# Attention with two mixtures of experts: pinned splits and swaps, value products four head pairs behind the scores

## The chip, the cores and the metric

One core of a Trainium2 chip runs the kernel. Its time is the device time of one execution in microseconds (us); the number for the kernel before is the median of 3 executions. The core has five engines that run at the same time and meet through semaphores: TensorE (PE, matmuls and transposes; its weight loads are shown as PEld), VectorE (DVE), ScalarE (ACT), GpSimd (POOL) and SyncE (SP), which computes nothing and issues DMAs in the order of its queue. TensorE's granted clock is shown as a share of 2.4 GHz; it is either 1.00 or 0.50.

## The reference

```python
# q, k, v: (4, 8, 576, 64); window 128; H = 8 heads, D = 64
scores = scale * q @ k^T                      # per batch and head
scores = where(0 <= i - j < 128, scores - slope[h] * |i - j|, -1e9)
attn = softmax(scores); x = attn @ v          # x becomes (2304, 512)
p = domain_probs / (sum(domain_probs) + 1e-9) # 4 experts, dense
out = sum_e p[:, e] * (relu(x @ w1[e]) @ w2[e])
logits = out @ phi                            # soft mixture: 8 experts, 4 slots each
d = softmax(logits, over tokens); slots = d^T @ out
slot_out[e] = relu(slots[e] @ m1[e]) @ m2[e]
result = softmax(logits, over slots) @ slot_out
```

## The kernel before, in words

The 2304 tokens are 18 tiles of 128. In float16 terms every operand is kept as a high half and a low half (the rounded value and the rest), so that the matmuls run in float16 and keep most of float32's precision.

**Attention, tiles 0 to 17.** For tile i, raw q, k and v (128 x 512, float32) are loaded by SyncE (`ld`, L292). ScalarE writes the high half of q and of k (`sp_qk_hi`, L300), GpSimd the low half (`sp_qk_lo`, L305). The halves lie in one buffer per name (`qs`, `ks`, one buffer each), so the split of the next tile can't begin before the DMA that transposes this tile's has landed. From tile 2 on, that transpose is a DMA issued by SyncE (`tr_q`, `tr_k` and `trans`, L318 to L338; L320 is the issue). qT needs a second copy with its halves exchanged: two VectorE copies (`swap_q`, L339 to L342). Tiles 0 and 1 are transposed by TensorE instead.

The heads go in four pairs per tile; `n = 4 i + hp` is the step of the main loop (L499), and "pair 12.1" below is tile 12, head pair 1. A step computes the scores (`qk`, L349, matmuls of L357 with qT and of L362 with the swapped qT, into one of two PSUM banks, S0 and S1 in turn). Then `soft` (L366): VectorE adds the bias and takes the row's extreme (L374, twice), ScalarE takes the exponential (L379, twice) and writes the high half of the probabilities (L384), GpSimd the low half (L385), and SyncE issues the DMA transpose to eT. `pv` (L392) multiplies eT with v (L402), LAG = 3 steps after the scores. After a tile's fourth pair, `xn` (L405) scales by the row sums, and `xn_c` (L432) splits the result (ACT, POOL) and has it transposed by a DMA into xT, which the first mixture's layer 1 reads.

**The first expert in the gaps.** Between the steps, pieces of the first mixture's expert 0 are put in from a list (`pend`) with a budget of modelled time per step: layer 1 (`l1_piece`, L199) reads xT, VectorE and ScalarE split its result (L213, L214), layer 2 is L227. Tiles 0 and 1 use float32 matmuls (L266, L276).

**After the attention** come the other experts (L634 and L709), then the soft mixture with its own weights and the output.

**What sets the order.** The kernel's text only says what is to be done. A scheduler orders each engine's instructions by the order of the text and by when its own model of time holds them ready, so one engine's order may differ from the text. Each engine then takes its list strictly in that order: an instruction that waits holds up everything behind it on its engine. `tc.issue_after(ins)`, which the change uses, makes instructions of a block stand behind `ins` on `ins`'s engine.

## Time and profile before

| | |
|---|---|
| median of 3 executions | 940.98 us (938.55 to 941.99) |
| the profiled execution | 940.18 us, span 938.3 us |
| mean granted clock of TensorE | 0.983 |
| TensorE busy | 886.7 us of the span (95%) |
| VectorE, ScalarE, GpSimd busy | 566.5, 372.4, 179.9 us |

The page cuts the span into 40 slices of 23.5 us. TensorE is at four and six tenths in the first two slices, at eight in five of the next nine, and at seven in two of the last three. The DMA engines are busy at six tenths or more through the first ten slices and nearly idle from the twelfth to the thirty-first. So there are three parts to read apart: the start and the attention (to about 260 us), the dense experts, and the soft mixture at the end. A busy share alone tells little here; the views that say what TensorE waited for, and when its clock was low, tell more.

### The profile page before, as it was taken

The numbers are of one execution on the slowest core, as the hardware profiler recorded it, in microseconds if no ns is written. First come the engines' busy times: TensorE is split into PE (matmuls) and PEld (weight loads), VectorE is DVE, ScalarE is ACT, GpSimd is POOL, SyncE is SP. The second block draws the span as 40 slices with busy tenths as digits, with TensorE's granted clock in tenths as the row PEclk, the third lists the DMA queues.
The fourth block names the chain that finished last, engine by engine and source line by source line (L and its number), as shares of the span: only waits on it lengthen the run. The fifth ranks groups of instructions, "written<-read, shape, count | busy, mean of one in ns | idle before, by whom it ended". The sixth has DMA issues, their size and how long they took to land.

```text
span 938.3 us, 16272 instructions
## 1 busy us (share of the span) xinstructions
PE 886.7 (95%) x6426; PEld 516.8 (55%) x6426; DVE 566.5 (60%) x1217; ACT 372.4 (40%) x912; POOL 179.9 (19%) x169
## 2 busy tenths in 40 slices
PE   4689898989899999999999999999999999999797
PEld 3566676656765655555555555555555445554432
DVE  7855565547549387657575756666666454556512
ACT  5956766757734243223131323232233201223412
POOL 5555655656520000000000000000000005310000
PEclk9989999999999999999999999999999999999799
DMA  9698998999960110100101010101001008983696
GB/s 261 124 192 157 178 191 174 185 199 152 147 142 24 46 46 3 44 23 23 45 1 45 1 46 1 45 3 44 23 23 46 0 1 303 221 216 133 237 377 241
DMA packets 222028, 102.35 MB, mean 109 GB/s; under 512 B 187216, under 2 KB 201584, under 8 KB 221952
## 3 DMA queue, kind: packets, MB, share of 16 engines
q1 hardware_dynamic: 212320, 78.14, 39.2%
q10 hardware_dynamic: 6800, 13.11, 4.0%
q0 software_dynamic: 2832, 10.07, 2.9%
q8 instruction: 50, 0.82, 0.4%
q14 instruction: 26, 0.21, 0.1%
HBM read 64.59 MB, written 4.72 MB: 74 GB/s over the span
## 4 chain that ended last, share of the span: by engine, by line
PE 75%; DMA 9%; ACT 4%; issue 4%; DVE 4%; POOL 2%; SPq 1%; POOLq 0%; DVEq 0%; ACTq 0%
PE l L709 22%; PE A L634 12%; PE l L199 9%; PE l L227 9%; PE C L634 6%; DMA eT<-e 4%; PE B L634 3%; PE hp L1040 2%; DMA qT<-qs 2%; PE l2f L276 2%; PE so_ps L1058 2%; PE x L402 1%; DMA m<-in_moe_w_dram 1%; ACT e L379 1%; PE fp L1071 1%
## 5 line engine op out<-in xcount | busy, mean ns | idle before, releaser
L709 PE MATMUL l<-w,h 128*128 128x512 f16 x1080 | 252.9, 379 | 0.0
L237 DVE SCALAR_TENSOR_TENSOR acc<-l,pr,acc 128x512 f32<-128x512 f32 x216 | 161.3, 748 | 126.6 <-PE l L709 103.3
L634 PEld LDWEIGHTS <-w 128*128 128x128 f16 x1260 | 123.1, 98 | 94.2
L709 PEld LDWEIGHTS <-h 128*128 128x128 f16 x1080 | 105.5, 98 | 115.3
L199 PE MATMUL l<-xT,w 128*128 128x256 f16 (+2 forms) x1152 | 149.4, 281 | 5.8 <-DMA xT<-xs 3.6
L227 PE MATMUL l<-w,h 128*128 128x512 f16 x600 | 141.9, 383 | 0.7 <-DVE acc L237 0.7
L658 ACT ACTIVATE ct<-A 128x384 f32<-128x384 f32 x90 | 43.5, 487 | 219.0 <-PE A L634 218.9
L199 PEld LDWEIGHTS <-w 128*128 128x128 f16 x1152 | 105.0, 99 | 39.4 <-issue 6.7
L803 POOL DMA_DIRECT2D m<-in_moe_w_dram x19 | 13.7, 723 | 510.2 <-DVE h L654 446.9
L385 POOL TENSOR_TENSOR e<-e,e 128x512 f16<-128x512 f32 (+1 forms) x72 | 80.9, 1130 | 61.8 <-ACT e L384 45.8
L227 PEld LDWEIGHTS <-h 128*128 128x128 f16 x600 | 57.8, 99 | 61.4 <-issue 3.5
L213 ACT ACTIVATE h<-l 128x256 f16<-128x256 f32 (+2 forms) x96 | 36.4, 382 | 110.2 <-PE l L199 75.9
L379 ACT ACTIVATE e<-e,nmx 128x256 f32<-128x256 f32 (+1 forms) x144 | 69.7, 485 | 20.2 <-DVE nmx L374 19.8
L214 DVE SCALAR_TENSOR_TENSOR h<-l,h 128x256 f16<-128x256 f32 (+2 forms) x96 | 40.9, 429 | 59.2 <-ACT h L213 59.0
L634 PE MATMUL C<-xs,w 128*128 128x384 f16 x360 | 71.3, 326 | 0.0
L374 DVE CUSTOM_DVE_ANT_0 e<-s,bias 128x256 f32<-128x256 f32 (+1 forms) x144 | 52.5, 404 | 28.4 <-PE s L362 23.5
L634 PE MATMUL A<-xs,w 128*128 128x384 f16 x360 | 69.3, 326 | 0.0
L634 PE MATMUL A<-xT,w 128*128 128x384 f16 x360 | 67.7, 327 | 0.0
L653 ACT ACTIVATE h<-ct 128x384 f16<-128x384 f32 x90 | 43.8, 515 | 46.5 <-PE l L709 25.1
L357 PE MATMUL s<-kT,qT 128*128 128x128 f16 x272 | 45.4, 228 | 7.7 <-DVE nmx L374 4.6
L654 DVE SCALAR_TENSOR_TENSOR h<-ct,h 128x384 f16<-128x384 f32 x90 | 47.6, 549 | 2.3 <-ACT h L653 2.1
L362 PE MATMUL s<-kT,qT 128*128 128x128 f16 x272 | 44.9, 230 | 4.0 <-DVE qT L342 4.0
(185 smaller groups left out, 993.2 us busy)
## 6 DMA issues: line engine op xcount, KB each, us to landing
m<-in_moe_w_dram ACTq DMA_DIRECT2D x25, 512.0 KB, 5.6
stg<-in_moe_w_dram SPq DMA_DIRECT2D x20, 512.0 KB, 4.9
m<-in_moe_w_dram SPq DMA_DIRECT2D x20, 512.0 KB, 10.2
m<-in_moe_w_dram POOLq DMA_DIRECT2D x19, 512.0 KB, 12.4
stg<-in_moe_w_dram SPq DMA_DIRECT2D x24, 256.0 KB, 3.2
out_dram<-ots SPq DMA_DIRECT2D x18, 256.0 KB, 3.0
qr<-in_q_dram SPq DMA_DIRECT2D x16, 256.0 KB, 3.9
kr<-in_k_dram SPq DMA_DIRECT2D x16, 256.0 KB, 4.3
```

The lines of the kernel that those rows point to most:

```text
L199: nc.tensor.matmul(pt, lhsT=w1_ap(e, fc, wa, kc), rhs=x_ap(t0, n, xa, kc), start=first_mm, stop=(kc == KC - 1 and wa == 1))
L227: nc.tensor.matmul(pt, lhsT=ht[:, ha, o:o + P], rhs=w2_ap(e, fc, wa), start=(fc == fcs[0] and ha == 0 and wa == 0), stop=(fc == fcs[-1] an ...
L237: nc.vector.scalar_tensor_tensor(out=a, in0=pt, scalar=p, in1=a, op0=ALU.mult, op1=ALU.add)
L357: nc.tensor.matmul(o, lhsT=qT[i][:, 0, h], rhs=mv, start=True, stop=False)
L362: nc.tensor.matmul(o, lhsT=qT[i][:, 1, h], rhs=mv, start=False, stop=True)
L374: nc.vector.tensor_tensor_reduce(out=et[:, hl, c0:], in0=st[:, hl, c0:], in1=bias[:, h, c0:], op0=ALU.add, op1=ALU.min, scale=-0.125, scal ...
L379: nc.scalar.activation(out=et[:, hl, c0:], in_=et[:, hl, c0:], func=AF.Exp, scale=-1.0, bias=nmx[i][:, h:h + 1], accum_out=sums[i][:, h:h ...
L385: nc.gpsimd.tensor_tensor(out=e2[:, :, 1], in0=et[:, :, c0:], in1=e2[:, :, 0], op=ALU.subtract)
L634: nc.tensor.matmul(o, lhsT=wq_[:, blk, wa, kc], rhs=xf(xa, kc), start=(first and kc == 0 and wa == 0 and xa == 0), stop=(kc == 1 and wa == 1),
L653: nc.scalar.activation(out=o[:, 0], in_=src, func=AF.Relu)
L654: nc.vector.scalar_tensor_tensor(out=o[:, 1], in0=src, scalar=0.0, in1=o[:, 0], op0=ALU.max, op1=ALU.subtract)
L709: nc.tensor.matmul(pt, lhsT=u["h"][:, z, ha, par, i * P:(i + 1) * P], rhs=w2_ap(e, 2 * qd + z, wa), start=(z == 0 and ha == 0 and wa == 0) ...
```

## The change

The edits, all in the attention stage:

- raw q, k and v share one ring of five buffers (`raw`) in place of two each; the scratch for the bias shares the ring of `e`;
- `soft` becomes three functions, called apart: the scores' extreme, the exponential with the halves, and the transpose;
- q's swap stands behind the extreme of head pair 2 (pinned on VectorE);
- the high half of the next tile's k stands behind the high half of pair 0's probabilities (pinned on ScalarE), one step earlier in the text than before; that of the q of the tile after the next stands behind pair 3's, which is also one step earlier; their low halves on GpSimd follow in the text;
- q's transpose moves from the tile's second step to its first, k's from the third to the second;
- `xn_f` and `xn_c` come at the end of a step; the pieces of the experts alternate with the value products in the text;
- LAG is 4 in place of 3, `e2` has four buffers in place of three, `eT` seven in place of six;
- a finished tile's expert pieces become available one step later.

```diff
-            t = at([P, H, D], F32, nme + "r")
+            t = at([P, H, D], F32, "raw", 5)
...
-    def soft(i, hp, st):
+    def soft_max(i, hp, st):
         kb0 = kbs(i)[0]
         if hp == 0:
             sums[i] = at([P, H], F32, "sums")
             nmx[i] = at([P, H], F32, "nmx")
-        c0, w = kb0 * P, (2 - kb0) * P
-        et = at([P, 2, 2 * P], F32, "e", 3)
+        c0 = kb0 * P
+        et = es[i, hp] = at([P, 2, 2 * P], F32, "e", 3)
         for hl in range(2):
             h = 2 * hp + hl
-            nc.vector.tensor_tensor_reduce(out=et[:, hl, c0:], in0=st[:, hl, c0:], in1=bias[:, h, c0:],
-                                           op0=ALU.add, op1=ALU.min, scale=-0.125, scalar=3.0e38,
-                                           accum_out=nmx[i][:, h:h + 1])
+            mx = nc.vector.tensor_tensor_reduce(out=et[:, hl, c0:], in0=st[:, hl, c0:], in1=bias[:, h, c0:],
+                                                op0=ALU.add, op1=ALU.min, scale=-0.125, scalar=3.0e38,
+                                                accum_out=nmx[i][:, h:h + 1])
+        return mx.ins
+
+    def soft_exp(i, hp):
+        kb0 = kbs(i)[0]
+        c0 = kb0 * P
+        et = es.pop((i, hp))
         for hl in range(2):
             h = 2 * hp + hl
             nc.scalar.activation(out=et[:, hl, c0:], in_=et[:, hl, c0:], func=AF.Exp, scale=-1.0,
                                  bias=nmx[i][:, h:h + 1], accum_out=sums[i][:, h:h + 1])
-        e2 = at([P, 2, 2, 2 * P], F16, "e2", 3)
+        e2 = at([P, 2, 2, 2 * P], F16, "e2", 4)
         if kb0:
             e2 = e2.rearrange("p a b c -> p (a b c)")[:, 0:4 * P].rearrange("p (a b c) -> p a b c", a=2, b=2)
-        nc.scalar.activation(out=e2[:, :, 0], in_=et[:, :, c0:], func=AF.Copy)
+        es[i, hp] = e2
+        eh = nc.scalar.activation(out=e2[:, :, 0], in_=et[:, :, c0:], func=AF.Copy)
         nc.gpsimd.tensor_tensor(out=e2[:, :, 1], in0=et[:, :, c0:], in1=e2[:, :, 0], op=ALU.subtract)
-        nb = 4 * w // P
-        eTt = at([P, 8, P], F16, "eT", 6)
-        trans(eTt[:, 0:nb], e2.rearrange("p a b c -> p (a b c)"), nb, i < 2)
+        return eh.ins
+
+    def soft_tr(i, hp):
+        nb = 4 * len(kbs(i))
+        eTt = at([P, 8, P], F16, "eT", 7)
+        trans(eTt[:, 0:nb], es.pop((i, hp)).rearrange("p a b c -> p (a b c)"), nb, i < 2)
         eT[i, hp] = eTt
...
-    scr = at([P, 2 * P], F32, "scr", 1)
+    scr = at([P, 2, 2 * P], F32, "e", 3)[:, 0]
...
-    LAG = 3
+    LAG = 4
...
-        avail.append((pvt(4 * tl[-1] + 3) + (3 if tl[-1] > 1 else 2 if tl[-1] else 1), tl))
+        avail.append((pvt(4 * tl[-1] + 3) + (4 if tl[-1] > 1 else 2 if tl[-1] else 1), tl))
...
-        if n < NS:
-            st = qk(i, hp)
-        for m in done:
-            if m % 4 == 3:
-                xn(m // 4)
-        if n < NS:
-            soft(i, hp, st)
-        for m in done:
-            if m % 4 == 3:
-                (xn_f if m < 8 else xn_c)(m // 4)
-            if m in (7, 9):
-                xn_h((m - 7) // 2)
-        if n < NS:
+        live = n < NS
+
+        if live:
+            mx = soft_max(i, hp, qk(i, hp))
+        for t in done:
+            xn(t)
+        if live and j < NT:
+            if hp == 2:
+                with tc.issue_after(mx):
+                    swap_q(j)
+            elif hp == 3:
+                sp_v_lo(j)
+
+            if j == 1:
+                if hp == 0:
+                    sp_qk_hi("q", 1)
+                    sp_qk_lo("q", 1, nc.gpsimd)
+                elif hp == 1:
+                    tr_q(1, True)
+                    sp_qk_hi("k", 1)
+                    sp_qk_lo("k", 1, nc.gpsimd)
+                elif hp == 2:
+                    tr_k(1, True)
+            elif hp == 0:
+                tr_q(j)
+            elif hp == 1:
+                tr_k(j)
             if hp < 3 and i + 2 < NT:
                 ld(i + 2, "qkv"[hp])
-            if i + 1 < NT:
-                if hp == 0:
-                    sp_qk_hi("q", i + 1)
-                    sp_qk_lo("q", i + 1, nc.gpsimd)
-                elif hp == 1:
-                    tr_q(i + 1, i + 1 < PE_T)
-                    sp_qk_hi("k", i + 1)
-                    sp_qk_lo("k", i + 1, nc.gpsimd)
-                elif hp == 2:
-                    tr_k(i + 1, i + 1 < PE_T)
-                    swap_q(i + 1)
-                    sp_v_hi(i + 1)
-                else:
-                    sp_v_lo(i + 1)
+        if live:
+            eh = soft_exp(i, hp)
+            if hp == 0 and 1 < j < NT:
+                with tc.issue_after(eh):
+                    sp_qk_hi("k", j)
+                sp_qk_lo("k", j, nc.gpsimd)
+            elif hp == 2 and j < NT:
+                sp_v_hi(j)
+            elif hp == 3 and i + 2 < NT:
+                with tc.issue_after(eh):
+                    sp_qk_hi("q", i + 2)
+                sp_qk_lo("q", i + 2, nc.gpsimd)
+            soft_tr(i, hp)
+        for t in done:
+            (xn_f if t < 2 else xn_c)(t)
+        if n in (9, 11):
+            xn_h((n - 9) // 2)
...
+        pvs = [m for m in range(NS) if pvt(m) == n]
         while pend and budget > 0:
             c, f = pend.pop(0)
             budget -= c
             f()
-        for m in range(NS):
-            if pvt(m) == n:
+            if pvs:
+                m = pvs.pop(0)
                 pv(m // 4, m % 4)
+        for m in pvs:
+            pv(m // 4, m % 4)
```

How the change moves instructions is shown at three places around tile 12. In the names, the numbers count tiles as the program makes them.

SyncE's queue before, where the probabilities of pair 11.3 (eT_464) and 12.0 (eT_473) are sent to be transposed; kT_490 and qT_482 are tile 13's, kT_527 tile 14's:

```order
L320 DMA_TRANSPOSE kT_490_2994<-ks_483_2930 128x8x128
L320 DMA_TRANSPOSE qT_482_2928<-qs_475_2877 128x8x128
L320 DMA_TRANSPOSE xT_321_1953<-xs_465_2823 128x8x128
L297 DMA vr_526_3221<-in_v_dram 128x8x64
L320 DMA_TRANSPOSE eT_464_2821<-e2_463_2818 128x8x128
L320 DMA_TRANSPOSE eT_473_2873<-e2_472_2870 128x8x128
L320 DMA_TRANSPOSE kT_527_3223<-ks_518_3167 128x8x128
```

Tile 13's k and q, an xT and a load stand ahead of pair 11.3.

SyncE's queue in the changed program at the same place: eT_458 is pair 11.3, eT_473, eT_482, eT_489 and eT_495 are pairs 12.0 to 12.3, qT_469 and kT_479 tile 13's:

```order
L320 DMA_TRANSPOSE xT_330_1972<-xs_474_2840 128x8x128
L320 DMA_TRANSPOSE eT_458_2776<-e2_456_2770 128x8x128
L320 DMA_TRANSPOSE qT_469_2826<-qs_457_2773 128x8x128
L297 DMA raw_486_2934<-in_v_dram 128x8x64
L297 DMA raw_504_3060<-in_q_dram 128x8x64
L320 DMA_TRANSPOSE eT_473_2838<-e2_471_2832 128x8x128
L320 DMA_TRANSPOSE kT_479_2884<-ks_472_2835 128x8x128
L297 DMA raw_513_3107<-in_k_dram 128x8x64
L320 DMA_TRANSPOSE eT_482_2893<-e2_481_2890 128x8x128
L320 DMA_TRANSPOSE eT_489_2943<-e2_487_2938 128x8x128
L320 DMA_TRANSPOSE eT_495_2993<-e2_493_2987 128x8x128
```

Pair 11.3 now goes ahead of tile 13's k and q; tile 13's q follows at once, and tile 13's k follows pair 12.0.

VectorE's list before, at the extremes of pair 12.2 (e_486) and 12.3 (e_495); qT_482 is tile 13's and L341, L342 its swap:

```order
L374 ISA e_486_2982,nmx_470_2864<-s_485_2973,bias_4_90 128x256
L374 ISA nmx_470_2864 128x1
L374 ISA e_486_2982,nmx_470_2864<-s_485_2973,bias_4_90 128x256
L374 ISA nmx_470_2864 128x1
L341 COPY qT_482_2928<-qT_482_2928 64x1024
L214 SCALAR_TENSOR_TENSOR h_450_2729<-l1_484_2933,h_450_2729 128x256
L342 COPY qT_482_2928<-qT_482_2928 64x1024
L374 ISA e_495_3026,nmx_470_2864<-s_492_3012,bias_4_90 128x256
```

The swap stands between the two pairs, with a result of layer 1 (L214) inside it.

VectorE's list in the changed program, at the same two pairs (e_485 and e_492) and the swap of tile 13's qT_469:

```order
L374 ISA e_485_2929,nmx_465_2817<-s_484_2920,bias_4_90 128x256
L374 ISA nmx_465_2817 128x1
L374 ISA e_492_2981,nmx_465_2817<-s_491_2972,bias_4_90 128x256
L374 ISA nmx_465_2817 128x1
L374 ISA e_492_2981,nmx_465_2817<-s_491_2972,bias_4_90 128x256
L374 ISA nmx_465_2817 128x1
L214 SCALAR_TENSOR_TENSOR h_462_2792<-l1_490_2945,h_462_2792 128x256
L341 COPY qT_469_2826<-qT_469_2826 64x1024
L342 COPY qT_469_2826<-qT_469_2826 64x1024
```

The swap stood ahead of the extreme of pair 12.3 and now stands behind it.

ScalarE's list before, at the exponentials of pairs 12.1 (e_478) and 12.2 (e_486); ks_518 is tile 15's k and qs_510 tile 14's q:

```order
L379 ACTIVATE e_478_2916,sums_469_2863<-e_478_2916,nmx_470_2864 128x256 x2
L213 ACTIVATE h_450_2729<-l1_484_2933 128x256
L302 ACTIVATE ks_518_3167<-kr_481_2926 128x8x64
L384 ACTIVATE e2_479_2921<-e_478_2916 128x2x256
L302 ACTIVATE qs_510_3112<-qr_474_2875 128x8x64
L379 ACTIVATE e_486_2982,sums_469_2863<-e_486_2982,nmx_470_2864 128x256 x2
```

Two splits stand between the exponentials of the two pairs.

ScalarE's list in the changed program from pair 12.1 (e_478) to 12.3 (e_492); qs_494 is tile 14's q:

```order
L385 ACTIVATE e_478_2881,sums_464_2816<-e_478_2881,nmx_465_2817 128x256
L385 ACTIVATE e_485_2929,sums_464_2816<-e_485_2929,nmx_465_2817 128x256
L213 ACTIVATE h_462_2792<-l1_490_2945 128x256
L385 ACTIVATE e_485_2929,sums_464_2816<-e_485_2929,nmx_465_2817 128x256
L391 ACTIVATE e2_481_2890<-e_478_2881 128x2x256
L385 ACTIVATE e_492_2981,sums_464_2816<-e_492_2981,nmx_465_2817 128x256 x2
L391 ACTIVATE e2_487_2938<-e_485_2929 128x2x256
L213 ACTIVATE h_462_2792<-l1_496_2995 128x256
L391 ACTIVATE e2_493_2987<-e_492_2981 128x2x256
L302 ACTIVATE qs_494_2990<-raw_470_2828 128x8x64
```

The split of tile 14's q now comes behind the last pair's high half, and no split of k is near.

## Rows read from the trace of the kernel before

**Rows 1.** Busy time by stretch: start:end, its length, each engine, granted clock, DMA

```profile
75.00:260.00 185.00, 168.71 (x1921) 123.50 (x1921) 106.58 (x360) 127.02 (x375) 108.57 (x93) 0.97 1.03 176
260.00:760.00 500.00, 500.00 (x2818) 270.67 (x2817) 323.53 (x551) 150.46 (x314) 6.07 (x6) 1.00 0.11 31
```

**Rows 2.** What TensorE waited for from 75 to 260 us: total, times, longest

```profile
PE x L402 <- DMA eT<-e: 9.6, 9, 2.3
PE l L199 <- DMA xT<-xs: 3.6, 2, 2.6
PE l L199 <- DVE h L214: 2.2, 1, 2.2
PE s L357 <- DMA qT<-qs: 0.7, 1, 0.7
```

**Rows 3.** Busy time of the four stretches that hold a low clock before 260 us

```profile
45.00:57.00 12.00, 8.63 (x59) 6.38 (x60) 10.66 (x37) 10.77 (x33) 8.11 (x7) 0.57 1.00 191
110.00:115.00 5.00, 4.24 (x36) 2.78 (x36) 2.85 (x13) 4.46 (x17) 4.46 (x4) 0.66 1.00 190
151.00:156.00 5.00, 4.28 (x25) 3.13 (x25) 2.02 (x4) 1.32 (x3) 1.78 (x2) 0.66 0.71 145
202.00:207.00 5.00, 5.00 (x26) 2.88 (x25) 4.42 (x13) 2.86 (x9) 2.71 (x2) 0.66 1.06 219
```

**Rows 4.** Two of TensorE's waits in the first 75 us

```profile
PE s L357 <- DVE nmx L374: 4.6, 5, 3.3
PE s L362 <- DVE qT L342: 4.0, 3, 2.0
```

**Rows 5.** Waits of VectorE and ScalarE for DMAs, 75 to 260 us

```profile
DVE qT L341 <- DMA qT<-qs: 19.1, 11, 3.9
...
ACT qs L302 <- DMA qT<-qs: 10.8, 6, 2.9
ACT e L384 <- DMA eT<-e: 10.2, 13, 2.3
...
ACT ks L302 <- DMA kT<-ks: 6.4, 6, 2.4
```

**Rows 6.** One of SyncE's own waits, 75 to 260 us

```profile
SPq L320 <- PE s L362: 14.8, 10, 4.3
```

**Rows 7.** SyncE's timeline: start, duration (us), what is issued

```profile
185.99 2.32 SPq L320 DMA_TRANSPOSE kT<-ks  x1
188.41 1.25 SPq L320 DMA_TRANSPOSE qT<-qs  x1
189.75 1.30 SPq L320 DMA_TRANSPOSE xT<-xs  x1
191.14 0.53 SPq L297 DMA_DIRECT2D vr<-in_v_dram  x1
191.77 4.12 SPq L320 DMA_TRANSPOSE eT<-e  x2
```

**Rows 8.** Timeline of all engines, 193 to 198 us; in brackets the idle time before

```profile
193.66 0.63 ACT L302 ACTIVATE qs<-qr 128x512 f16<-128x512 f32 x1 [2.00 <-DMA qT<-qs]
193.67 0.42 DVE L341 COPY qT<-qT 64x1024 f16<-64x1024 f16 x1 [3.91 <-DMA qT<-qs]
...
194.37 1.15 POOL L307 TENSOR_TENSOR qs<-qr,qs 128x512 f16<-128x512 f32 x1 [0.88 <-ACT qs L302]
194.57 1.23 DVE L342 COPY qT<-qT 64x1024 f16<-64x1024 f16 x1
...
197.58 0.52 PE L402 MATMUL x<-vv,eT 128*128 128x64 f16 x12 [1.34 <-DMA eT<-e]
```

**Rows 9.** The chain of waits: start, duration (us), TensorE's matmuls without pause

```profile
258.65 2.59 PE l L227 x12
261.24 0.35 PE x L402 x12
...
262.04 1.31 PE l L199 x12
```

More of the change, by code (lines that the diff above doesn't have):

```diff
@@ L500 @@
         i, hp = divmod(n, 4)
-        done = [m for m in range(NS) if pvt(m) == n - 1]
+        j = i + 1
+        done = [m // 4 for m in range(NS) if pvt(m) == n - 1 and m % 4 == 3]
         if n == 4:
```

## The prediction

> **What bounds the kernel now.** I began with the busy time by stretch. After 260 us TensorE is busy without a break for 500 us [rows 1], so a microsecond that it saves ahead of 260 us shifts everything behind it. From 75 to 260 us it is busy for 168.7 of 185 us at a mean clock of 0.97. Next come its waits in that stretch: 9.6 us for the transposed probabilities in nine waits, 3.6 for xT, 2.2 for a result of layer 1 that VectorE had not read, 0.7 for q [rows 2], 16.1 us together. Then the clock: three 5 us stretches at 0.66 lose 5 x 0.34 = 1.7 us each, 5.1 us, and 45 to 57 us at 0.57 loses 12 x 0.43 = 5.2 us [rows 3]. So the attention stage offers 16.1 + 5.1 = 21.2 us, and the start a little more [rows 4].
>
> The reader is then to see why the probabilities are late. The chain of a pair is extreme, exponential, high half, low half, transpose, and each step is done by an engine that takes its list in order. VectorE stood 19.1 us, 3.9 at the longest, at the swap of a q that had not landed; ScalarE stood 10.8 and 6.4 us at the splits of q and k, whose one buffer was still being read by a transpose, and 10.2 at the high half, whose three buffers were [rows 5]. SyncE stood 14.8 us until scores let go of a q or k buffer [rows 6]. One place shows all of it. Tile 13's k took 2.32 us in SyncE's queue, its q, an xT and a load of v another 1.25, 1.30 and 0.53, and only then did two probability transposes go [rows 7]. When q landed, VectorE had idled 3.91 us and ScalarE 2.00, and TensorE waited 1.34 us for the first of those probabilities [rows 8].
>
> **The change part by part.** No arithmetic is added or removed, so TensorE's own work is unchanged; what counts is order. The name of the lag promises more work between a pair's scores and its value product. I counted it in the two TensorE lists, with 0.029 us per value matmul, 0.109 per layer-1 and 0.216 per layer-2 matmul [rows 9]. Over tiles 7 to 17 it is 11.2 us on the mean before and 11.2 after; 11.7 to 10.7 for a tile's first pair, 11.1 to 11.4 for the other three. So I price the lag at nothing: the scheduler had already put the products where it held them ready. The extra buffers of e2 and eT and the pins can gain only by making the chain shorter.
>
> - *Probabilities.* In the new SyncE queue pair 11.3 has the xT (1.30) ahead of it and no longer k, q and v: 2.32 + 1.25 + 0.53 = 4.1 us fewer [rows 7]. Pair 12.0 has 11.3, q and two loads ahead, about 2 x 1.28 + 2 x 0.53 = 3.6, where k, q, xT, v and 11.3 made 6.7. The nine waits were 2.3 us at most [rows 2], less than what goes. Not all of it will go: SyncE needs per tile 7 transposes x 1.28 + 3 loads x 0.55 = 10.6 us [rows 7], and TensorE's work per tile, counted as above from tile 7 to 17, is 11.4, so the queue is 93% full if TensorE never waits. Bounds: 0 and 9.6; I take 6.0, nearer to the upper, since the queue shown is the row at hand.
> - *xT.* By the lists, between the last value product of tile 7 and the first layer 1 that reads it lie 12.8 us of work, where 6.1 lay; for tile 5 it is 9.1 after 8.8. The longer wait, 2.6 us, goes, and the other 1.0 stays [rows 2]. Bounds 0 and 3.6; I take 2.6.
> - *Swap and q.* The swap stands behind the extreme of pair 3 in the list, with pair 0's and the next tile's k's transposes issued since that of its q, so VectorE does not stand there; the layer-1 result (2.2) that was queued behind the swap is read at once, and q is there for the scores (0.7). Bounds 0 and 2.9; I take 2.9. Queued behind the pinned swap are layer-1 and layer-2 results and the row sums; if q were late, they and so PSUM would wait as before.
> - *Splits of q and k.* Pinned behind a high half, they come when the last transpose of their buffer is nearly a tile old, so 10.8 + 6.4 us of ScalarE's waits go. ScalarE is busy 127 of 185 us [rows 1]; by itself this is worth nothing, and its share lies in the first item.
> - *Clock.* Two of the three low stretches go with the waits ahead of them: 2 x 1.7 = 3.4 us. Bounds -1.7 (one more) and 5.1.
> - *Start.* Tile 2's second extreme follows the first directly, where a weight split stood between, and tile 3's second half of scores stands behind eight float32 matmuls. Of the waits of 4.6 and 4.0 us [rows 4] I take 1.5. Bounds: -1 (the ring of five lets the sixth raw load go only when q's first buffer is free) and 5.
> - *New waits* that I can't see, bounded by nothing and 4.4 (twice the one wait of another kind [rows 2]): 2.2 back.
>
> Sum: 6.0 + 2.6 + 2.9 + 3.4 + 1.5 - 2.2 = 14.2 us. The profiled execution took 940.2 us (0.8 below the median shown, 1.9 above its span): 940.2 - 14.2 = **926.0 us**.
>
> Two places where a rule weighs against this. The second swap copy took 1.23 us beside a GpSimd instruction of 1.15, the first, alone, 0.42 [rows 8]; the pin puts both copies beside GpSimd's low halves of pairs 2 and 3. At 0.8 us per copy that is at most 1.6 us x 15 tiles = 24 us of VectorE, which is busy 106.6 of 185 [rows 1], so nothing in the sum. The Trainium skill's page "SBUF — State Buffer", section "SBUF: two separate sides", says that VectorE in a two-port mode and GpSimd lock their shared ports against each other for the whole instruction. The row agrees; by the rule GpSimd is held too, 0.4 us per copy, which the sum can bear.
>
> The low clock at 202 us comes after waits such as the 1.34 us that ended at 197.58 [rows 3, 8], but thirteen waits from 75 to 260 us came with only three low stretches [rows 2, 3]. The Trainium skill's page "TensorE: Matmul & The Clock Gate", section "HAM oscillation — how this bites in real kernels", says that the price of a re-throttle is paid again after each long enough wait. By that rule the clock term is 5.1 if all such waits go and 0 if as many stay, and the sum 924.3 or 929.4.
>
> **The rivals.**
> 1. *SyncE's queue becomes the bound.* For it: 10.6 of 11.4 us per tile, and its DMAs fill the 16 engines (share 1.03 [rows 1]). Against: it stood 14.8 us for buffers [rows 6]. The 13.5 tiles of this stretch (counted in TensorE's list) take 13.7 us each now; were the queue to hold them at 13.2, 13.5 x 0.5 = 6.8 us come: 933.4.
> 2. *The waits only change their name*: probabilities in time, but scores or layer 1 late, since all is as close-set as before. For it: the same 11.2 us between. Against: 61 us of waits on other engines should end [rows 5, 6]. 938 to 942, 940.
> 3. *Slower: a tile's first pair.* Its product stands 1.0 us sooner behind its scores (10.7 after 11.7), and k's splits and transpose now follow on its heels. It decides if the first pair's chain stays over 10.7 us: 1.0 x 14 tiles = 14 us more waiting, two more low stretches 3.4, less swap and start 4.4: 953. Against: its own place in SyncE's queue improves by 3.1 us.
> 4. *Everything goes*: 16.1 + 5.1 + 1.5 = 22.7: 917.5.
>
> **How the numbers follow.** Forecast 0.60 (its own range 920 to 932), rival 1 0.15, rival 2 0.11, rival 3 0.08, rival 4 0.06. What a measurement here can tell from no change is about 0.5%, 4.7 us, so faster means below 936.3: 0.60 + 0.06 + 0.14 = 0.80; same 0.12; slower 0.08. The range 917 to 938 leaves out rival 3, most of rival 2 and half of rival 4.
>
> **What would show it right or wrong.** Right: VectorE's waits at the swap under 3 us in sum, ScalarE's at the splits of q and k under 3; TensorE's for probabilities near 3.6, for xT near 1; one low stretch between 75 and 260 us; and that stretch's work some 13 us shorter. Rival 1 would show probabilities late with SyncE issuing without a pause; rival 3 waits at the first value product of most tiles. Wrong altogether: the attention stage shorter, but a wait after 260 us that eats it.

## The result, and the profile after

The changed kernel took 947.9 us (median of 4, 946.7 to 948.4) against 941.5 for the kernel before beside it: 1.0076 of its time, 95% interval 1.0053 to 1.0098. The forecast was 926.0, the range 917 to 938, and slower had a chance of 0.08. Its profiled execution took 946.66 us, 6.5 more than that of the kernel before.

The busy time by stretch, of the changed kernel; first the stretch of [rows 1], then its three low-clock stretches, which answer to [rows 3]. The column after the five engines is TensorE's granted clock.

```profile
75.00:260.00 185.00, 165.32 (x1851) 118.60 (x1850) 105.52 (x346) 121.79 (x363) 105.45 (x94) 0.95 1.07 180
148.00:155.00 7.00, 6.05 (x42) 3.58 (x43) 1.77 (x14) 3.73 (x16) 2.45 (x3) 0.51 1.04 217
199.00:206.00 7.00, 5.12 (x26) 3.42 (x27) 4.76 (x9) 1.64 (x3) 2.70 (x3) 0.52 1.15 213
253.00:258.00 5.00, 4.49 (x41) 2.53 (x42) 2.75 (x9) 1.69 (x6) 1.63 (x2) 0.66 1.16 200
```

TensorE is idle for 19.7 us of the stretch, where it was 16.3. There are still three low stretches, but two are 7 us long: 7 x 0.49 + 7 x 0.48 + 5 x 0.34 = 8.5 us are lost, where it was 5.1. These two differences, 3.4 and 3.4, are 6.8 us; the profiled executions differ by 6.5. The clock's share doesn't hang on one execution: the granted clock was 0.978 in the mean of the four executions, and 0.981 to 0.982 in the sets of 13 to 35 of the kernel before that ran beside the experiments; that difference alone is 2 to 4 us. The first 75 us are as before (51.3 us busy, 51.4 before), and from 260 to 760 us TensorE is busy without a break, as before.

What TensorE waited for between 75 and 260 us (total us, times, longest), the answer to [rows 2]:

```profile
PE x L412 <- DMA eT<-e: 10.7, 11, 2.7
PE s L362 <- DVE qT L342: 3.6, 2, 2.3
PE s L357 <- DMA kT<-ks: 2.5, 2, 1.6
PE s L357 <- DMA qT<-qs: 1.2, 2, 0.9
PE l L199 <- DMA xT<-xs: 1.2, 1, 1.2
PE s L357 <- DVE nmx L374: 0.3, 1, 0.3
```

The probabilities are waited for about as long as before (9.6 us); new is 7.3 us for the next tile's q, k and swap, where there was 0.7. The same stretch on VectorE, ScalarE and SyncE's queue, the answer to [rows 5, 6]:

```profile
DVE qT L341 <- DMA qT<-qs: 18.4, 10, 5.0
...
ACT e L391 <- DMA eT<-e: 2.7, 2, 2.2
...
ACT qs L302 <- DMA qT<-qs: 0.2, 1, 0.2
```
```profile
SPq L320 <- POOL e L392: 38.4, 34, 3.0
SPq L320 <- POOL ks L307: 12.6, 7, 3.8
SPq L320 <- POOL qs L307: 12.1, 10, 3.2
```

ScalarE's 17.2 us at the splits are gone, and SyncE's 14.8 us for buffers that scores held. But VectorE still stands 18.4 us at the swap, and SyncE now stands 24.7 us for the low halves of q and k, where it was 10.7. SyncE's queue before:

```profile
SPq L320 <- POOL e L385: 34.1, 31, 3.3
...
SPq L320 <- POOL ks L307: 6.9, 6, 1.4
...
SPq L320 <- POOL qs L307: 3.8, 4, 1.5
```

One place shows how the work now comes late. In the kernel before, the high half of tile 13's q was written at 174 us (ScalarE, timeline):

```profile
174.46 0.63 ACT L302 ACTIVATE qs<-qr 128x512 f16<-128x512 f32 x1
```

In the changed kernel it comes 13 us later (tile 12's first scores come 4.6 us later), behind the high half of pair 11.3, where it is pinned (timeline of all engines):

```profile
187.14 0.62 ACT L391 ACTIVATE e<-e 128x512 f16<-128x512 f32 x1
...
187.66 0.62 ACT L302 ACTIVATE qs<-raw 128x512 f16<-128x512 f32 x1
...
188.44 1.15 POOL L392 TENSOR_TENSOR e<-e,e 128x512 f16<-128x512 f32 x1
...
189.56 1.15 POOL L307 TENSOR_TENSOR qs<-raw,qs 128x512 f16<-128x512 f32 x1
...
189.63 2.58 SPq L320 DMA_TRANSPOSE xT<-xs  x1
...
192.32 1.25 SPq L320 DMA_TRANSPOSE eT<-e  x1
...
193.68 2.19 SPq L320 DMA_TRANSPOSE qT<-qs  x1
...
197.30 0.52 PE L412 MATMUL x<-vv,eT 128*128 128x64 f16 x12 [1.46 <-DMA eT<-e]
...
198.10 1.15 POOL L392 TENSOR_TENSOR e<-e,e 128x512 f16<-128x512 f32 x1 [1.99 <-ACT e L391]
...
198.16 1.37 DVE L341 COPY qT<-qT 64x1024 f16<-64x1024 f16 x1 [4.96 <-DMA qT<-qs]
198.18 0.23 PE L357 MATMUL s<-kT,qT 128*128 128x128 f16 x1 [0.36 <-DMA qT<-qs]
...
199.21 1.34 POOL L307 TENSOR_TENSOR qs<-raw,qs 128x512 f16<-128x512 f32 x1
199.54 1.28 DVE L342 COPY qT<-qT 64x1024 f16<-64x1024 f16 x1
...
200.88 0.29 PE L362 MATMUL s<-kT,qT 128*128 128x128 f16 x1 [2.32 <-DVE qT L342]
```

Read it downwards: high half, low half behind another pair's on GpSimd, SyncE's queue behind an xT and a probability, 2.3 us to land, two slow copies beside GpSimd. VectorE has stood 4.96 us; TensorE loses 1.46 + 0.36 + 2.32 = 4.1 us, and the clock falls at 199 us. The reader is to see that none of this work was done ahead: each engine takes it up only when its queue comes to it, and nothing is in hand.

Over tiles 5 to 17, from the times of the trace: k landed 3.4 us after the tile before it had its first scores and was wanted 12.8 us after them; now 11.6 and 13.4. The swap was done 9.0 us after the last scores of the tile before last and wanted at 15.8; now 16.7 and 19.0. The scores of a tile, spread over 10.2 us before (first to last pair, mean of 12 tiles), now come within 5.6 us, with 8.4 us to the next tile's.

### The profile page after: what moved, and what is told of

The parts are those of the page before. It is cut to its first block, busy times and chain, and to the rows that moved or that the text cites. A ratio compares the mean times of both kernels' runs of the same rounds, so it can differ in the third digit from the quotient of the medians.

```text
span 944.9 us, 16275 instructions
## 1 busy us (share of the span) xinstructions
PE 889.4 (94%) x6426; PEld 519.2 (55%) x6426; DVE 567.7 (60%) x1217; ACT 370.8 (39%) x912; POOL 177.0 (19%) x169
## 4 chain that ended last, share of the span: by engine, by line
PE 74%; DMA 6%; ACT 3%; DVE 2%; SPq 2%; issue 1%; POOL 1%; ACTq 0%; POOLq 0%; DVEq 0%
PE l L740 25%; PE A L665 12%; PE l L227 9%; PE l L199 9%; PE C L665 6%; PE B L665 3%; PE hp L1071 2%; DMA eT<-e 2%; PE so_ps L1089 2%; DMA qT<-qs 1%; PE fp L1102 1%; DMA raw<-in_v_dram 1%; ACT e L385 1%; DMA m<-in_moe_w_dram 1%; PE x L412 1%
## 5 line engine op out<-in xcount | busy, mean ns | idle before, releaser
L834 POOL DMA_DIRECT2D m<-in_moe_w_dram x19 | 13.7, 723 | 511.6 <-DVE h L685 448.2
L214 DVE SCALAR_TENSOR_TENSOR h<-l,h 128x256 f16<-128x256 f32 (+2 forms) x96 | 40.8, 427 | 43.9 <-ACT h L213 43.4
L412 PE MATMUL x<-vv,eT 128*128 128x64 f16 x816 | 40.5, 197 | 16.0 <-DMA eT<-e 10.7
## 6 DMA issues: line engine op xcount, KB each, us to landing
m<-in_moe_w_dram SPq DMA_DIRECT2D x20, 512.0 KB, 10.2
```

Of the source, the lines that this page charges most:

```text
L412: nc.tensor.matmul(o, lhsT=t[:, (hl * 2 + ea) * nk + kb - kb0], rhs=vvs[i - 1 + kb][:, h, va], start=(kb == kb0 and ea == 0 and va == 0), ...
```

## The experiments

Ratios are to the kernel before, run beside each, with the 95% interval. "q and k" below is what TensorE waits for q, k and the swap between 75 and 330 us, "idle" all that it stands there. All are gathered in a table at the end.

**One part undone.** First the pins:

```diff
-                with tc.issue_after(mx):          # swap_q(j)
-                with tc.issue_after(eh):          # sp_qk_hi("k", j)
-                with tc.issue_after(eh):          # sp_qk_hi("q", i + 2)
+                if True:                          # in all three places
```

> The changed kernel with its three pins taken off (the swap may again be placed anywhere in VectorE's queue, the halves of q and k anywhere in ScalarE's); all else as changed. The changed kernel took 947.9 us against 941.5. Theory 1 (the pins make the order bad: the pinned swap moves tile 3's last scores behind the FP32 expert pieces, whose scores then end at 66.0 instead of 52.7 us, and holds up the fourth pair's extremes for up to 4.8 us): 942 us or less, with tile 4's first scores back near 75 us (80.8 in the changed kernel). Theory 2 (SyncE's queue: the probabilities stand there 4 to 8 us behind other transposes whatever the pins do): within 2 us of the changed kernel, 946 to 950, with the stretch from GpSimd's low half to the end of the issue still above 3.5 us in tiles 5 to 12. Theory 3 (the lag of four is the loss): unchanged as well, 946 to 950.

Measured 939.8 us, 0.9993 (0.9979 to 1.0007). Without pins the loss is gone, and tile 4's first scores end at 76.1 us, as theory 1 has it. (The next run has them at 83.5 us and no loss, so these scores are not what costs.)

```diff
-    LAG = 4
+    LAG = 3
-    ... (4 if tl[-1] > 1 else 2 if tl[-1] else 1), tl))
+    ... (3 if tl[-1] > 1 else 2 if tl[-1] else 1), tl))
```

> The changed kernel with value products three head pairs behind the scores, as before the change (the expert's tiles become due three pairs on too); pins, buffers and the order of the code as changed. Theory 3 (a lag of four does not make the distance on TensorE longer, but bunches the scores in twos and threes, so that their transposes queue on SyncE): 941 to 944 us, with fewer waits for eT between 75 and 260 us than the 10.7 us of the changed kernel. Theory 1 (pins): 946 to 950, since tile 3's last scores stay behind the FP32 pieces. Theory 2 (SyncE's queue): 946 to 952, the distance being shorter and the queue as long.

Measured 938.7 us, 0.9977 (0.9964 to 0.999). The loss goes here too, so neither has it alone; but the waits for eT did not shrink as theory 3 wanted (11.2 us), and the time lies below its bracket.

```diff
-            if pvs:                   # after the first piece
-                m = pvs.pop(0)
-                pv(m // 4, m % 4)
         for m in pvs:                 # behind the loop over pend: stays
             pv(m // 4, m % 4)
```

> The changed kernel with the value product put after all of a step's expert pieces, as before the change, and not after the first of them; all else as changed. Theory 1 (pins) and theory 2 (SyncE's queue): 946 to 950 us, no difference. Theory 4 (putting the value product after the first piece takes away the cover that the other pieces gave it, as the slack between landing and use, 0 to 2 us in tiles 6 to 8, would have it): 942 to 944, with the waits for eT between 75 and 260 us at 5 us or less instead of 10.7.

Measured 945.7 us, 1.0067 (1.0046 to 1.0088): theory 4 falls, though the waits for eT went down to 6.8 us.

```diff
-                nc.sync.dma_start(out=t[off:off + n], ...
+                (nc.gpsimd if i > 1 else nc.sync).dma_start(out=t[off:off + n], ...
```

> The changed kernel with the loads of q, k and v from tile 2 on issued from GpSimd's queue and not from SyncE's; all else as changed. It takes three issues of 0.5 to 0.6 us per tile, 1.7 of about 10.6 us, off SyncE and puts three onto GpSimd, which is busy less than half of its time there. Theory 2 (SyncE's queue is what makes the probabilities late): 940 to 944 us, with the stretch from GpSimd's low half to the end of SyncE's issue down from 4 to 8 us to 2 to 4 us in tiles 5 to 12. Theories 1, 3 and 4 (pins, lag, place of the value product): 946 to 950, no difference; slower than that if GpSimd's issues are longer than SyncE's and hold its low halves up.

Measured 954.3 us, 1.0156 (1.0126 to 1.0185), outside theory 2's bracket. As the cause of the loss theory 2 had fallen with the first run, where from the low half to the end of the issue it is still 4.1 us and the loss is gone. This run is no clean test of it. The queue did get shorter (3.8 us in the mean, then 2.7), but a transpose took longer to land (2.4, then 3.4), and an issue takes GpSimd 0.87 to 0.89 us in the mean, where SyncE's took 0.69. GpSimd was not busy less than half of the time before it got these issues, as the expectation has it, but 105 of 185 us. And of the 6.4 us behind the changed kernel 5.0 are idle time of TensorE in the first 75 us (28.7, where it was 23.7). Lines of GpSimd (busy us, mean ns):

```profile
L297 POOL DMA_DIRECT2D raw<-in_k_dram x13 | 11.5, 888 | 1.9 <-DVE r L418 1.3 <-POOL ks L307 0.6
L297 POOL DMA_DIRECT2D raw<-in_v_dram x13 | 11.3, 871 | 5.2 <-DVE r L418 3.4 <-DVE h L214 1.8
L297 POOL DMA_DIRECT2D raw<-in_q_dram x12 | 10.4, 867 | 0.3 <-POOL qs L307 0.3
```

**Which pin.** With `issue_after(eh)` removed twice, the swap's pin kept:

> The changed kernel without the pins of q's and k's high halves; the swap's pin and all else as changed. Without any pin it took 0.9993 of the time before, with all pins 1.0076. In the written order the work that TensorE has between a pair's scores and its value product is 11.8 us in the mean over tiles 4 to 17 in the changed kernel, and 13.3 without the pins of the halves. Theory 1a (the halves' pins are the loss: they hold the high halves behind the exponentials, so that TensorE's order has the scores later and the cover of four pairs is lost again): 938 to 942 us, waits for eT between 75 and 260 us under 9. Theory 1b (the swap's pin is the loss: the fourth pair's extremes stand behind a swap that waits for q): 946 to 950 us, as with all pins.

Measured 939.0 us, 0.999 (0.9977 to 1.0003), as theory 1a has it. What TensorE waits for between 75 and 330 us:

```profile
PE x L412 <- DMA eT<-e: 7.9, 10, 2.5
PE l L199 <- DMA xT<-xs: 2.3, 2, 1.2
PE s L362 <- DVE qT L342: 1.6, 3, 0.7
PE l L199 <- DVE h L214: 1.5, 2, 1.0
```

With `issue_after(mx)` removed, the halves' pins kept:

> The changed kernel without the pin of q's swap; the pins of the high halves and all else as changed. The written cover between scores and value product is 11.9 us, as with the pin (11.8). Theory 1a (the halves' pins are the loss): 946 to 950 us. Theory 1b (the swap's pin is the loss): 939 to 942 us, and the waits of the first pair's scores for the swap, 3.6 us between 75 and 260, gone.

Measured 942.9 us, 1.0024 (1.0011 to 1.0036), between the theories: the halves' pins cost without the swap's, less than with it. The waits for the swap did not go (4.7 us between 75 and 260 us).

**The lag.** All pins off at a lag of three:

> The changed kernel with a lag of three and without any pin: what is left of the change is the code in its new order, the buffers, and the place of the value product. With a lag of three and all pins it took 0.9977 of the time before. Theory 1a (pins and lag of four work against each other, each harmless by itself): 936 to 942, about as with the lag of three alone. If the pins were bad by themselves, it is faster than that, 933 to 937; if they were worth something at a lag of three, slower, 941 to 944.

Measured 938.5 us, 0.9974 (0.9962 to 0.9986), as theory 1a has it. Then the lag, with its buffers, on the kernel before:

```diff
-    LAG = 3
+    LAG = 4
-        e2 = at([P, 2, 2, 2 * P], F16, "e2", 3)
+        e2 = at([P, 2, 2, 2 * P], F16, "e2", 4)
-        eTt = at([P, 8, P], F16, "eT", 6)
+        eTt = at([P, 8, P], F16, "eT", 7)
...
```

> The kernel before with a lag of four, four and seven buffers for the probabilities and one ring of five for the loads, but with none of the rest (no pin, old order of the code, value product behind the expert's pieces). The written cover rises from 11.5 to 13.3 us. If the lag is worth what its cover promises: the waits for eT between 75 and 260 us fall from 9.6 to 3.6 us or less, and with them some of the low clock: 931 to 936 us. If the cover is eaten up elsewhere (SyncE's queue, fewer buffers for the loads): 939 to 944 us.

Measured 939.6 us, 0.9996 (0.9986 to 1.0007). The lag with its buffers buys nothing, and its waits between 75 and 330 us show where the gain went:

```profile
PE l L199 <- DVE h L214: 9.2, 5, 3.8
PE x L402 <- DMA eT<-e: 4.4, 6, 2.0
```

The waits for eT fall from 9.6 to 4.4 us as the cover promises, and those for layer 1's results rise from 2.2 to 9.2 [rows 2]: the waits change their name.

**Earlier, later, and the ring.** The halves, pins and all:

```diff
-            if hp == 0 and 1 < j < NT:            # k of j
-            elif hp == 3 and i + 2 < NT:          # q of i + 2
+            if hp == 3 and i + 2 < NT:            # k of i + 2
+            elif hp == 2 and i + 2 < NT:          # q of i + 2
```

> The changed kernel with all pins and a lag of four, but the high and low halves of q and k one head pair earlier (q's behind the third pair's exponentials of the tile before last, k's behind the fourth's); all else as changed. Read from the trace of the changed kernel, in the mean over tiles 5 to 17: k lands 11.6 us after the first scores of the tile before it, and TensorE wants it 13.4 us after them (before the change 3.4 and 12.8); q is swapped 16.7 us after the last scores of the tile before last and wanted 19.0 us after them (before 9.0 and 15.8). Theory L (the pins tie the next tile's q and k to this tile's scores by a path as long as a tile takes, so that nothing is in hand and each delay is handed on): one pair earlier gives 3 us in hand for both, 938 to 941 us, waits for q, k and the swap between 75 and 260 us under 3 instead of 7.6, and less than 10 us of low clock there instead of 17. Theory P (pins in themselves, by the order they force on ScalarE's and VectorE's queues): 945 to 950.

Measured 939.1 us, 0.9975 (0.9963 to 0.9987). The time and the waits are as theory L has them, its path is not: k has 1.8 us in hand and the swap 2.7, hardly more than before the move (1.8 and 2.3), while SyncE now takes 5.3 us and not 3.8 from a pair's low half to the end of its issue. So the mean lead doesn't explain why the loss is gone. What went are the waits for the swap, and 13.7 us of low clock (17.1, now 3.4); those for eT grew. TensorE's waits there:

```profile
PE x L412 <- DMA eT<-e: 13.4, 17, 2.4
PE s L357 <- DMA kT<-ks: 1.6, 2, 0.9
PE l L199 <- DMA xT<-xs: 0.9, 2, 0.6
```

```diff
-            t = at([P, H, D], F32, "raw", 5)
+            t = at([P, H, D], F32, nme + "r")
-        eTt = at([P, 8, P], F16, "eT", 7)
+        eTt = at([P, 8, P], F16, "eT", 6)
```

> The changed kernel with two buffers each for the loads of q, k and v, as before the change, in place of one ring of five; to make room the transposed probabilities have six buffers and not seven. Theory L: the ring is not the cause, 944 to 950 us, and k still lands 11 to 12 us after the first scores of the tile before it. Theory R (with a ring of five the loads stand in SyncE's queue until a buffer is free, and the transposes behind them): 939 to 943.

Measured 943.7 us, 1.0028 (1.0016 to 1.004): between the two; k still lands 11.6 us after the first scores. Whether the ring has a share of 4 us, or the order or the sixth buffer that came with it, it doesn't tell.

The swap's pin alone at a lag of three:

> The changed kernel with a lag of three and the pin of q's swap alone, without the pins of the halves. With a lag of three and all pins it took 0.9977 of the time before, without any pin 0.9974; with a lag of four and the swap's pin alone 0.9990. Theory L: the leads of q and k stay open without the halves' pins, and the swap's pin alone costs nothing: 936 to 940 us. If the swap's pin costs by itself at either lag: 941 to 944.

Measured 942.4 us, 1.0007 (0.9992 to 1.0021), in the second theory's bracket, but not told apart from the kernel before. Then the later halves at a lag of three:

```diff
-            elif hp == 0:
+            elif hp == 1:
                 tr_q(j)
-            elif hp == 1:
+            elif hp == 2:
                 tr_k(j)
...                                  # halves: q(j) behind eh of pair 0, k(j) behind eh of pair 1
```

> The kernel with a lag of three and all pins (0.9977 of the time before), with the halves of q one head pair later (behind the first pair's exponentials of the tile before its own) and those of k one later (behind the second pair's), with their transposes one step later too: the double dose for theory L. From the rows of the changed kernel the path from a tile's first scores to the next tile's swapped q is then about 15 us (3.5 to the first pair's high half, 2 for q's high half, 2.2 for its low, 3.6 on SyncE, 2.3 to land, 1.6 for the swap), where TensorE has 11.4 us of work per tile. Theory L: each of about 13 tiles lasts 2 to 4 us longer, 965 to 995 us. Theory P (pins by themselves, wherever they stand): 937 to 945, about as with the lag of three.

Measured 940.4 us, 0.9993 (0.9977 to 1.0009): theory L's price falls. The lateness is there (in 9 of 13 tiles k has under 0.7 us in hand, in 11 the swap), and TensorE waits 8.5 us for q and k; but it waits only 5.8 for eT, so that late q and k are no loss by themselves:

```profile
PE x L412 <- DMA eT<-e: 5.8, 5, 1.6
PE s L362 <- DVE qT L342: 4.2, 6, 1.4
PE s L357 <- DMA kT<-ks: 3.7, 4, 1.4
```

**Chance of the order, or the edits.** Numbers that are no part of the change:

```diff
-        budget = min(budget + 2000.0, 5000.0)
+        budget = min(budget + 1960.0, 5000.0)     # or 2050.0
-        avail.append((pvt(4 * tl[-1] + 3) + (4 if tl[-1] > 1 ...
+        avail.append((pvt(4 * tl[-1] + 3) + (5 if tl[-1] > 1 ...   # the third run alone
```

> The changed kernel with one number altered that is no part of the change: each head pair is granted 1960 and not 2000 ns of the expert's pieces. All edits of the change stand; TensorE's order is the same until the eighth tile or so and differs in places behind. So far every undoing of one part of the changed kernel (1.0076 of the time before) gave a faster one, by 2 to 9 us, whichever part it was. Theory C (no part costs: the loss is how the waits happen to fall in this one order, in clusters that also hold the clock low): 938 to 945 us. Theory M (pins of the halves together with a lag of four cost, in any order): 945 to 950.

> As the run with 1960, with 2050 ns granted per head pair. Theory C (chance of the order): 938 to 945 us, and the idle time and the low clock between 75 and 330 us differ from those of the run with 1960. Theory M (pins of the halves and a lag of four): 945 to 950.

> The changed kernel with the expert's tiles due five steps and not four behind a tile's last value product; the lag between scores and value product and all else as changed. Theory C (chance of the order): 938 to 945 us. Theory M (pins of the halves and a lag of four): 945 to 950.

> The kernel before with 2050 in place of 2000 ns of the expert's pieces per head pair, and nothing of the change: how far an alteration of the order alone moves the kernel before. Theory C: it moves it by some us as well, to 936 to 946 us (941 before). Theory M: within 2 us of 941.

Measured 945.1 (1.0048, 1.003 to 1.0066), 945.6 (1.0053, 1.0037 to 1.0069) and 947.6 us (1.0079, 1.006 to 1.0097), and 939.6 (0.9986, 0.9972 to 0.9999) for the kernel before. Theory C falls: the changed kernel is slower in each of four orders (the first of these runs lies on the border of the two brackets, the others in theory M's). What TensorE waits for wanders; with 2050, between 75 and 330 us, it is k:

```profile
PE s L357 <- DMA kT<-ks: 8.1, 6, 2.2
PE x L412 <- DMA eT<-e: 4.9, 8, 1.1
PE s L362 <- DVE qT L342: 2.5, 4, 1.0
```

The later halves again, at a lag of four, and the last combination:

> The changed kernel with a lag of four and all pins, and the halves and transposes of q and k one head pair later (the same edit cost nothing at a lag of three: 0.9993 of the time before). Theory M (halves tied to this tile's own pairs cost at a lag of four, where the four pairs of scores of a tile run in a bunch of 5 us with 8 us between bunches): 947 to 956 us, idle time of TensorE between 75 and 330 us of 19 us or more. If what the halves have in hand does not matter even at a lag of four, and the loss comes from something else in the pair of edits: 939 to 944.

> A lag of three with the pins of the halves and without the swap's pin: the last of the eight combinations of lag, halves' pins and swap's pin. Theory M (halves' pins cost only with a lag of four): 936 to 941 us, 0.995 to 1.000 of the time before. If the halves' pins cost by themselves: 943 or more.

Measured 947.7 us, 1.0069 (1.0051 to 1.0087), as theory M expects, and 945.4, 1.0043 (1.0027 to 1.0059), against it: the halves' pins cost at a lag of three too, where the swap isn't pinned. With the later halves TensorE waits most for the swap:

```profile
PE s L362 <- DVE qT L342: 9.0, 8, 1.5
PE x L412 <- DMA eT<-e: 5.1, 4, 2.6
```

**Together.** us of TensorE between 75 and 330 us; "low" is time at the low clock there.

| kernel | ratio | q and k | idle | low |
|---|---|---|---|---|
| halves not pinned, or earlier | | | | |
| before | 1 | 0.7 | 16.3 | 10.2 |
| before, budget 2050 | 0.9986 | 2.5 | 14.6 | 13.7 |
| before, lag 4 | 0.9996 | 0.2 | 14.4 | 6.8 |
| lag 3, no pin | 0.9974 | 0.4 | 14.3 | 6.8 |
| lag 3, swap's pin | 1.0007 | 0.2 | 15.6 | 10.2 |
| lag 4, no pin | 0.9993 | 1.4 | 13.6 | 6.8 |
| lag 4, swap's pin | 0.9990 | 1.6 | 13.6 | 3.4 |
| lag 4, all, one pair earlier | 0.9975 | 1.6 | 16.0 | 3.4 |
| halves pinned where the change has them, or later | | | | |
| lag 3, halves' pins | 1.0043 | 3.4 | 19.9 | 6.8 |
| lag 3, all | 0.9977 | 2.0 | 15.3 | 3.4 |
| lag 3, all, later | 0.9993 | 8.5 | 16.9 | 6.8 |
| lag 4, halves' pins | 1.0024 | 7.0 | 17.3 | 10.2 |
| lag 4, all (the change) | 1.0076 | 7.3 | 19.7 | 17.1 |
| its value products as before | 1.0067 | 7.5 | 18.1 | 17.1 |
| its loads in six buffers | 1.0028 | 5.2 | 18.2 | 6.8 |
| its budget 1960 | 1.0048 | 11.1 | 17.6 | 10.2 |
| its budget 2050 | 1.0053 | 10.9 | 17.5 | 10.2 |
| its tiles due later | 1.0079 | 8.4 | 20.0 | 10.2 |
| its halves later | 1.0069 | 12.4 | 22.3 | 13.7 |
| its loads from GpSimd | 1.0156 | 4.3 | 20.8 | 10.2 |

Pinning the halves where the change has them, or one pair later, goes with waits for q and k of 7.3 us in the mean and 18.6 us of idle time, where the others have 1.1 and 14.8. The mean ratio is 0.9990 in the upper part (0.9974 to 1.0007) and 1.0042 in the lower without its last row. Most of the lower part is the changed kernel with one more edit, so these are not twelve independent trials. In the eight combinations of lag and pins the halves' pins cost 0.39% in the mean (+0.69, -0.30, +0.31, +0.86), the lag 0.20 (+0.19, -0.17, -0.19, +0.99) and the swap's pin 0.04; each mean is within the scatter of its four differences.

Shown, at a lag of four: with the halves pinned there every kernel is slower than the kernel before (nine, 1.0024 or more), and without these pins, or with them one pair earlier, none is (four, 0.9996 or less); no interval of the one group meets one of the other. Taking off the halves' pins alone takes the loss away, and so does a lag of three with all pins kept: in the changed kernel it takes both. Not shown is by what path. Late q and k alone are not it (8.5 us of waits and no loss at a lag of three with later halves), nor is the low clock alone (two kernels of the lower part, tiles due later and halves later, have a mean clock of 0.981 over their executions, as the kernel before, and lose 0.8 and 0.7%). Open as well: at a lag of three the halves' pins cost in one of three kernels only. With all pins it waits as little as the kernels of the upper part, though its k has 1.1 us in hand and its swap 2.2 (the changed kernel 1.8 and 2.3), and no run says why.

## Why the prediction was wrong

In the trace of the changed kernel the terms of the sum came out thus (us, gain positive):

| term | forecast | measured |
|---|---|---|
| Probabilities | 6.0 | 9.6 - 10.7 = -1.1 |
| xT | 2.6 | 3.6 - 1.2 = 2.4 |
| Swap and q | 2.9 | 2.2 + 0.7 - 1.2 = 1.7 |
| Clock | 3.4 | 5.1 - 8.5 = -3.4 |
| Start | 1.5 | 0 |
| New waits | -2.2 | -3.6 - 2.5 - 0.3 = -6.4 |
| sum | 14.2 | -6.8 |

Two steps failed, one for the sign and one for the size. The sum misses by 21.0 us: 7.1 at the probabilities, 6.8 at the clock, 4.2 at the new waits, 2.9 at the rest. Taking off the halves' pins gives back 0.86%, some 8 us; the other 13 us are gain that no kernel here shows (the best is 0.9974).

- *Splits of q and k*, priced at nothing, is the step that failed for the sign. ScalarE's 17.2 us went as said; but the item asked only what the splits wait for, not who waits for them. They had been done up to a tile early, and their waits were the price of being early. Such a pin holds the split back and never brings it forward: k lands 11.6 us and not 3.4 after the scores before it. Taking off these two pins alone restores 0.9990 (run with the swap's pin alone), and the waits for q, k and the swap fall from 7.3 to 1.6 us: that is where the new waits come from.
- *Probabilities* is the term mis-sized most: 6.0 forecast, -1.1 measured, and only 9.6 - 7.9 = 1.7 with the halves' pins off. The row of the queue was right for its place, but no forecast of the chain. The extremes and exponentials did come sooner (in the mean over tiles 5 to 16, 1.8 to 1.4 and 1.4 to 1.2 us), SyncE's part, from the low half to the end of the issue, grew from 3.1 to 3.8, and from scores to landing it is 12.0 us, where it was 11.8. That the scores now come within 5.6 us is not the reason: without the halves' pins they are spread over 8.5 us and SyncE's part is 3.8 too, and with the later halves at a lag of four they come within 4.9 us and it is 2.5. What makes it longer stays open. The sum for SyncE's queue was low as well: a transpose's issue took 1.47 us in the mean between 75 and 260 us and not 1.28, which makes 7 x 1.47 + 3 x 0.55 = 11.9 us per tile, more than TensorE's 11.4.
- *Lag at nothing*: right for the lag by itself, but wrong in reason, and wrong beside the pins. The order has 13.3 us between scores and value product with the lag alone (11.5 before, tiles 4 to 17) and 11.8 with the halves' pins, which take it back; the lag alone gained nothing either (0.9996). With all pins it costs: 1.0076 with a lag of four, 0.9977 with three.
- *Swap and q*: the layer-1 wait went as forecast; that VectorE would not stand at the swap was wrong (18.4 us). I counted the transposes ahead of q's in SyncE's queue, not when its low half would be there.
- *Clock*: the term took the low stretches to go with the waits ahead of them. The waits stayed, and the low time grew. The low stretch at 199 us begins among the 4.1 us of waits shown above; those at 148 and 254 among waits of 0.74, 0.85 and 1.39, and of 2.67 and 0.51 us. That is no rule: waits of 0.49, 0.25, 0.87 and 1.16 us between 120 and 126 us were followed by none. The Trainium skill's page "TensorE: Matmul & The Clock Gate", section "A second HAM failure mode: psum-queue depth-cycling", tells of a kernel whose short idles between groups of matmuls, frequent as they were, made the clock swing; the trace agrees in this, that none of its waits there is over 2.7 us.
- *xT* was right. *Start* gained nothing: the two waits of [rows 4] fell from 8.6 to 5.0 us, but TensorE's idle time in the first 75 us stayed (23.6, now 23.7).
- Rival 1 (SyncE's queue as the bound) did not come: it gave 933.4, and its sign, SyncE issuing without a pause, is not there, since SyncE stands 38.4 + 12.6 + 12.1 = 63 us for GpSimd's low halves. Rival 2 (the waits change their name, 938 to 942) is what the kernels without the halves' pins show (938.5 to 942.4). Rival 3 named the right sign and k's late transpose, but priced the first pair's product; its waits are at the next tile's first scores instead.

## What to carry to other kernels

An engine that waits early for a buffer is not losing time if nobody waits for it: before a wait off the path is removed by moving work later, ask how long its result lay ready, and who takes it next. A pin only ever delays the pinned instruction; before adding one, read from the trace when the pinned instruction ran and when its consumer wanted it. And where a scheduler orders everything, test an edit in two or three orders: here altered numbers that mean nothing moved the time by up to 0.3%. Three of these kernels (a lag of three without pins or with all, and the halves one pair earlier) beat the kernel before by 0.25% or so, with intervals that exclude 1, and the changed one by 1%; but 0.25% is no more than what those altered numbers moved, so whether their edits earn it is not shown.

## What the runs showed of the hardware

An issue of the same 256 KB load took GpSimd 0.87 to 0.89 us in the mean, SyncE 0.69 in the changed kernel (median 0.57), and with the loads moved to GpSimd transposes from SyncE landed 1.0 us later after their issue. The Trainium skill's page "DMA: Bandwidth & Descriptors", section "Issuing engines are not separate DMA queues", says that DMAs issued from several engines run on the same 16 DMA engines and save only issue time; the rows agree: from a low half to the end of its issue SyncE took 1.1 us less, and the landing, 1.0 us later, took that back.
